# The four token-mixing stages: one float32 product of unsplit operands for each three products of rounded halves

## The chip, the core and the metric

The kernel runs on one core of one Trainium2 chip. The metric is the device time of one execution, in microseconds (us). The engines that matter here are TensorE (PE, with its weight loads PEld), VectorE (DVE), ScalarE (ACT), GpSimd (POOL) and SyncE (SP), whose queue issues nearly all transfers (SPq in the rows).

## The reference

Three blocks follow each other, with B = 2 sequences, H = 8 heads, S = 768 positions, D = 64 (so C = 512 channels):

```python
# 1 attention: a window of 16 around each position, plus 24 block summaries (K: max, V: mean)
scores = concat([mask(q @ k.T / 8), q @ k_sum.T / 8 + log(32)]); a = softmax(scores)
x = (a @ concat([v, v_sum])).reshape(B, S, C)
# 2 mixer: over positions, then over channels
xt = x.transpose(0, 2, 1)
h = relu(xt @ w_tok1) @ w_tok2               # 768 -> 256 -> 768
u = x + h.transpose(0, 2, 1)
x = u + relu(u @ w_ch1) @ w_ch2              # 512 -> 1536 -> 512
# 3 normalisation and MLP
x = x + relu(layernorm(x) * g @ w_ch1) @ w_ch2   # 512 -> 2048 -> 512
```

The weights come as float64 and are turned into float32 in the kernel.

## The kernel before

**Attention** is cut into 24 quads (n = 0 to 23, three for each of the eight head pairs of both sequences; a sequence has 12). A quad makes its scores (PE, L284), subtracts mask and row extremum (DVE, L304), takes the exponential (ACT, L314), transposes (PE, L321), evacuates (ACT, L328), multiplies with V (PE, L341) and normalises into the tile `u`, which holds x for the whole kernel (DVE, L355 and L358). These products are float32.

**Every other product** is made of three products on operands of the rounded type `float32r`: an operand is kept as a rounded part (`h`) and the rest (`l`), and `mm3` (L196 to L200) adds h·h, h·l and l·h in PSUM. The splitting costs one copy (rounded part) and one subtraction (rest) per operand: for `u` in attention an ACT copy (L372, `xh`) and a POOL subtraction (L381, `xl`) per quad; for the hidden layer of token mixing an ACT Relu (L400, `hh`) and a DVE pass (L401, `hl`); for each half of a weight an ACT copy (L175, `wh`) and a DVE subtraction (L182, `wl`).

**Weights** come as 62 halves of 128x512. SP loads one into a `stage` buffer, of which there are three (L165); ACT takes the absolute value of its upper words (L113), and DVE puts the float32 together in four passes (L127, L129, L131, L135; the tile is `dec`). Then the split follows. This chain is a generator (`conversion`, L139) from which pieces are drawn: in attention `convert(ops)` weaves four, later two, DVE steps into each quad's normalisation. It stops when no slot is free. A slot holds two halves with both parts; there are three slots in attention, which is what the six halves of w_tok1 and w_tok2 fill, so no weight of the channel products is converted before attention has ended. Then eight slots are added, and later five more.

**Token mixing** has two stages per sequence. `g1` (L384) makes, for two halves of the channels and two tiles of the hidden layer, 6 products of 128x256 (8 such groups in all). `g2` (L404) makes, for each of 6 tiles of positions, 2 products of 128x512 and adds the result to `u` on DVE (L418; 12 groups). Those of sequence 0 and the g1 of sequence 1 are written into attention, from quad 9 on; the rest follows it, together with transposes of `u`.

**The order.** In attention each step of a quad is put at a due time (the table `ORDER` and the calls of `put`), and PE runs them in just that order. What the other engines run in what order is decided by the tile scheduler within what the program states. From the end of attention to the end, the channel products (`g3`, `g4`) take nearly all of PE, with conversions and transposes beside them.

A loop `fill` (L603) sends small products through PE in the first quads. It is not changed.

Of the kernel before, what the change touches and what calls it, by code (L numbers as in the profile page):

```python
# [52 lines left out]
class Kern:  # L53
# [311 lines left out]
    def att_hi(self, n):  # L365
        nc = self.nc
        i, qd = divmod(n, 3)
        b, p = divmod(i, NPAIR)
        x = self.u[:, b * ST + 2 * qd : b * ST + 2 * qd + 2, p * P : p * P + P]
        hf, c0 = p // 2, (p % 2) * P  # L370
        xh = self.xh[hf][:, 2 * qd : 2 * qd + 2, c0 : c0 + P]
        nc.scalar.copy(xh, x)  # L372

    def att_lo(self, n):
        i, qd = divmod(n, 3)
        b, p = divmod(i, NPAIR)
        hf, c0 = p // 2, (p % 2) * P
        x = self.u[:, b * ST + 2 * qd : b * ST + 2 * qd + 2, p * P : p * P + P]
        xh = self.xh[hf][:, 2 * qd : 2 * qd + 2, c0 : c0 + P]
        xl = self.xl[hf][:, 2 * qd : 2 * qd + 2, c0 : c0 + P]  # L380
        self.nc.gpsimd.tensor_tensor(xl, x, f32(xh), op=ALU.subtract)  # L381
# [465 lines left out]
```

## Time and profile before

| What | Value |
|---|---|
| Time, median of 3 runs | 602.31 us (601.63 to 602.54) |
| The profiled execution: its span (no other time is given of it) | 603.4 us |
| PE busy | 581.6 us, 96% |
| DVE busy | 336.3 us, 56% |
| ACT busy | 211.7 us, 35% |
| POOL busy | 43.6 us, 7% |
| Transfers in | 48.08 MB |

The slices of the profile (15 us each) show four stretches: loading and the first quads, where no engine is full; attention until about 100 us; the end of token mixing until about 128 us; and then 475 us in which PE is at 9 tenths or more. POOL works only in the first 105 us. The transfers run at 230 to 340 GB/s in the first 75 us and at about 100 GB/s after 105 us.

### The profile page before, as it was taken

To read this page: it belongs to the slowest core of one execution; us is meant where nothing else is said; L and a number is where in the kernel's file an instruction comes from. 1 tells how busy PE (TensorE), PEld (TensorE's weight loads), DVE (VectorE), ACT (ScalarE), POOL (GpSimd) and SP (SyncE) were. 2 spreads that over 40 slices of the span, in tenths; PEclk is the share of its full clock that TensorE was granted. 3 is DMA by queue.
4 is the path that set the end of the run, shared out by engine and by line. 5 is a ranking of instruction groups with operands and counts; after the bars stand their busy time and mean duration, and the time that the engine had idled before them with its cause. 6 is when DMAs were issued, how large, how long until landed. Compare 5 with 4: busy or idle time off the path is not lost.

```text
span 603.4 us, 9137 instructions
## 1 busy us (share of the span) xinstructions
PE 581.6 (96%) x3584; PEld 506.2 (84%) x3584; DVE 336.3 (56%) x848; ACT 211.7 (35%) x451; POOL 43.6 (7%) x78
## 2 busy tenths in 40 slices
PE   6777999999999999999999999999999999999997
PEld 2455777789899889899989998998988999989996
DVE  3698976998278899788799931111163211111122
ACT  3988878443233444333444411101122101011010
POOL 0544632000000000000000000000000000000000
PEclk8988999999999999999999999999999999999999
DMA  9979820335034333234323100000010100000011
GB/s 275 338 233 290 271 88 3 104 140 179 31 106 139 105 104 106 94 116 140 114 82 121 35 1 0 1 1 0 1 52 11 44 0 1 0 1 1 0 53 53
DMA packets 21505, 51.81 MB, mean 86 GB/s; under 512 B 2003, under 2 KB 8403, under 8 KB 21462
## 3 DMA queue, kind: packets, MB, share of 16 engines
q1 hardware_dynamic: 21456, 51.21, 26.3%
q8 instruction: 28, 0.46, 0.3%
q14 instruction: 15, 0.12, 0.1%
q10 hardware_dynamic: 6, 0.02, 0.0%
HBM read 48.08 MB, written 3.15 MB: 85 GB/s over the span
## 4 chain that ended last, share of the span: by engine, by line
PE 87%; DMA 5%; DVE 4%; ACT 2%; issue 1%; SPq 1%; DVEq 0%; ACTq 0%
DMA stage<-in_wts_dram 2%; PE g L198 2%; PE g L200 2%; PE g L199 2%; DMA Q<-in_q_dram 1%; DMA V<-in_v_dram 1%; PE av L341 1%; PE pt L321 1%; PE scores L284 1%; PE tx L502 1%; PE tu L435 1%; PE acc_('x', 2)_0_4718 L199 1%; PE acc_('x', 0)_0_3717 L199 1%; PE acc_('x', 2)_1_4719 L200 1%; PE acc_('x', 1)_0_3870 L199 1%; PE acc_('x', 2)_2_4720 L199 1%
## 5 line engine op out<-in xcount | busy, mean ns | idle before, releaser
L131 DVE SCALAR_TENSOR_TENSOR dec<-stage,dec 128x512 uint32<-128x512 uint32 x62 | 44.8, 723 | 0.8
L113 ACT ACTIVATE dec<-stage 128x512 f32<-128x512 f32 x62 | 41.9, 678 | 7.0 <-DMA stage<-in_wts_dram 6.8
L182 DVE TENSOR_TENSOR wl<-dec,wh 128x512 fp32r<-128x512 f32 x62 | 43.2, 699 | 0.0
L135 DVE SCALAR_TENSOR_TENSOR dec<-stage,dec 128x512 uint32<-128x512 uint32 x62 | 42.5, 686 | 0.8
L175 ACT CAST wh<-dec 128x512 fp32r<-128x512 f32 x62 | 38.1, 616 | 12.2 <-DVE dec L135 11.8
L314 ACT ACTIVATE pr<-sn,mn 128x120 f32<-128x120 f32 x96 | 30.8, 385 | 11.8 <-DVE mn L304 11.5
L129 DVE TENSOR_SCALAR dec<-dec 128x512 uint32<-128x512 uint32 x62 | 28.4, 458 | 0.9
L127 DVE TENSOR_SCALAR dec<-dec 128x512 f32<-128x512 f32 x62 | 27.8, 451 | 1.4 <-ACT dec L113 1.3
L284 PE MATMUL scores<-K,Q 64*64 64x120 f32 x384 | 16.7, 292 | 12.1 <-DVE mn L304 7.8
L284 PEld LDWEIGHTS scores<-K,Q 64*64 64x64 f32 x384 | 10.8, 141 | 19.5 <-DVE mn L304 10.5
L304 DVE CUSTOM_DVE_ANT_0 sn<-scores,mask 128x120 f32<-128x120 f32 x96 | 21.7, 274 | 5.5 <-PE scores L284 5.4
L381 POOL TENSOR_TENSOR xl<-u,xh 128x256 fp32r<-128x256 f32 x24 | 19.6, 818 | 27.6 <-ACT xh L372 27.6
L253 POOL TENSOR_TENSOR VT<-VT 128x384 f32<-128x384 f32 (+3 forms) x28 | 18.6, 664 | 30.7 <-DMA VT<-in_vt_dram 29.3
L321 PE MATMUL pt<-ident,pr 128*120 128x128 f32 x96 | 17.7, 308 | 1.0 <-ACT pr L314 1.0
L341 PEld LDWEIGHTS av<-V,PT 121*64 121x64 f32 x384 | 14.2, 145 | 5.3 <-issue 2.6
L341 PE MATMUL av<-V,PT 121*64 121x65 f32 x384 | 17.6, 237 | 0.5 <-POOL VT L253 0.3
L603 PE MATMUL warm_ps<-warm 128*128 128x512 bf16 x48 | 16.5, 455 | 1.2 <-DVE warm L665 1.2
L321 PEld LDWEIGHTS pt<-ident,pr 128*120 128x120 f32 x96 | 12.0, 150 | 6.0 <-ACT pr L314 2.4
L198 PE MATMUL g<-xh,wh 128*128 128x256 f32 x48 | 14.3, 299 | 0.5 <-DVE u L418 0.5
L328 ACT COPY PT<-pt 120x512 f32<-120x512 f32 x24 | 13.9, 579 | 0.4
L477 DVE TENSOR_SCALAR xn<-u,mv,rs 128x128 f32<-128x128 f32 x48 | 14.0, 342 | 0.0
L200 PE MATMUL g<-xh,wl 128*128 128x256 f32 x48 | 13.5, 282 | 0.0
(3004 smaller groups left out, 1677.0 us busy)
## 6 DMA issues: line engine op xcount, KB each, us to landing
stage<-in_wts_dram SPq DMA_DIRECT2D x62, 512.0 KB, 3.3
V<-in_v_dram SPq DMA_DIRECT2D x16, 306.0 KB, 9.0
K<-in_k_dram SPq DMA_DIRECT2D x8, 480.0 KB, 8.2
Q<-in_q_dram SPq DMA_DIRECT2D x8, 384.0 KB, 6.9
VT<-in_vt_dram SPq DMA_DIRECT2D x8, 384.0 KB, 8.2
out_dram<-u SPq DMA_DIRECT2D x12, 256.0 KB, 2.1
mask<-in_mask_dram SPq DMA_DIRECT2D x1, 240.0 KB, 5.3
ident<-in_ident_dram SPq DMA_DIRECT2D x1, 64.0 KB, 5.1
```

What stands on the lines that cost most here:

```text
L113: nc.scalar.activation(m, self.raw[n][:, :, 1].bitcast(F32), AF.Abs)
L129: nc.vector.tensor_scalar(mi, mi, 3, 0x3FFFFFF8, op0=ALU.logical_shift_left, op1=ALU.bitwise_and)
L131: nc.vector.scalar_tensor_tensor(mi, t[:, :, 1], 0xC0000000, mi, op0=ALU.bitwise_and, op1=ALU.bitwise_or)
L135: nc.vector.scalar_tensor_tensor(mi, t[:, :, 0], 29, mi, op0=ALU.logical_shift_right, op1=ALU.bitwise_or)
L175: self.nc.scalar.copy(self.slots[c if c < 16 else c - 16][0][:, s], x)
L182: self.nc.vector.tensor_tensor(wl[:, s], x, f32(wh[:, s]), op=ALU.subtract)
L199: nc.tensor.matmul(out, lhs[0], rhs[1], start=False, stop=False)
L200: nc.tensor.matmul(out, lhs[1], rhs[0], start=False, stop=last)
L284: nc.tensor.matmul(ps[cols, j, e, :NK], Q[rows, 64 * w : 64 * w + 64], K.rearrange("p v c -> p (v c)")[rows, a : a + NK], start=True, stop ...
L314: nc.scalar.activation(pr[:, u], sn[:, u], AF.Exp, bias=mn[:, u : u + 1], scale=-1.0)
L321: nc.tensor.transpose(ps[:NK, u * P : u * P + P], pr[:, u], self.ident)
L341: nc.tensor.matmul(ps[64 * j : 64 * j + 64, e, 65 * r : 65 * r + 65], pt[:, u * P + 64 * (r ^ j) : u * P + 64 * (r ^ j) + 64], V[:, j, 2 * ...
```

## The change

The token weights are decoded into six float32 tiles `tok` and not split; `u` is not split, and g1 reads it as it is; the hidden layer is kept as one float32 tile, made by one ACT Relu; g1 and g2 issue one float32 product where they issued three rounded ones. The tiles of the split parts fall away, and the space goes to slots: five instead of three in attention, then seven and later four. The slots now hold only channel weights, so `conversion` goes on to these (halves 6 to 15) within attention.

```diff
-NHALF = 2 * (3 + F1 + F2)
+NTOK = 6
+NHALF = NTOK + 2 * (F1 + F2)
+NSLOT = 16
...
+        to = self.tok[h].bitcast(U32) if h < NTOK else mi
         nc.vector.scalar_tensor_tensor(
-            mi, t[:, :, 0], 29, mi, op0=ALU.logical_shift_right, op1=ALU.bitwise_or
+            to, t[:, :, 0], 29, mi, op0=ALU.logical_shift_right, op1=ALU.bitwise_or
...
-            if 0 <= h < NHALF and not self.ready(h // 2):
+            if NTOK <= h < NHALF and not self.ready((h - NTOK) // 2):
...
     def split_hi(self, h):
+        if h < NTOK:
+            return
...
     def split_lo(self, h):
+        x = self.dec.pop(h) if self.wide else self.raw.pop(h)
+        if h < NTOK:
+            self.half[h] = self.tok[h]
+            return
...
     def g1(self, b, hf):
-                self.mm3(ps[:, :256], self.tok1(st, t), (xh[:, st], xl[:, st]), st == 0, st == ST - 1)
+                nc.tensor.matmul(
+                    ps[:, :256], self.tok1(st, t), self.u[:, b * ST + st, cs], start=st == 0, stop=st == ST - 1
+                )
             yield
-            nc.scalar.activation(hh, ps[:, :256], AF.Relu)
-            nc.vector.scalar_tensor_tensor(hl, ps[:, :256], 0.0, f32(hh), op0=ALU.max, op1=ALU.subtract)
+            nc.scalar.activation(self.h[b][:, t, cs], ps[:, :256], AF.Relu)
...
     def g2(self, b):
-                self.mm3(ps, self.tok2(t, st), (self.hh[b][:, t], self.hl[b][:, t]), t == 0, t == 1)
+                nc.tensor.matmul(ps, self.tok2(t, st), self.h[b][:, t], start=t == 0, stop=t == 1)
...
-            put(n + O["hi"], lambda n=n: self.att_hi(n))
-            put(n + O["lo"], lambda n=n: self.att_lo(n))
...
-        low = {x0: 5 + O["lo"], x1: 11 + O["lo"], w0: 17 + O["lo"], w1: 23 + O["lo"]}
+        low = {x0: 5 + O["norm"], x1: 11 + O["norm"], w0: 17 + O["norm"], w1: 23 + O["norm"]}
...
-        self.add_slots(slots_a, 3)
+        self.add_slots(slots_a, 5)
...
-        self.add_slots(slots_b, 8)
+        self.add_slots(slots_b, 7)
...
-                self.add_slots(slots_c, 4)
+                self.add_slots(slots_c, 2)
-                self.add_slots(slots_d, 1)
+                self.add_slots(slots_d, 2)
```

Three places show what this moves. Line numbers are each kernel's own: L284, L321, L341, L355, L358 and L304 of before are L298, L335, L355, L369, L372 and L318 of the changed kernel, and the decode passes L127, L129, L131, L135 are L129, L131, L133, L138.

PE, just after the value product of quad 15: the first group of g2 between two quads, before.

```order
L284 MATMUL scores<-K_100,Q_97 64x120 x8
L321 MATMUL pt_1068<-ident,pr_1015 120x128 x4
L341 MATMUL av_1073<-V_104,PT_101 64x65 x8
L198 MATMUL g_0_0_1098<-hh_118,wh_72 128x512
L199 MATMUL g_0_0_1098<-hl_120,wh_72 128x512
L200 MATMUL g_0_0_1098<-hh_118,wl_73 128x512
L198 MATMUL g_0_0_1098<-hh_118,wh_74 128x512
L199 MATMUL g_0_0_1098<-hl_120,wh_74 128x512
L200 MATMUL g_0_0_1098<-hh_118,wl_75 128x512
L284 MATMUL scores<-K_100,Q_97 64x120 x8
```

The same place of the changed kernel.

```order
L298 MATMUL scores<-K_104,Q_101 64x120 x8
L335 MATMUL pt_997<-ident,pr_957 120x128 x4
L355 MATMUL av_1002<-V_108,PT_105 64x65 x8
L397 MATMUL g_0_0_1026<-h_118,tok_123 128x512
L397 MATMUL g_0_0_1026<-h_118,tok_124 128x512
L298 MATMUL scores<-K_104,Q_101 64x120 x8
```

The quads stand where they stood; six rounded products have become two of float32.

DVE, around the normalisation of quad 5 (`rec` and `u` are its two passes, `dec` and `wl` a half's conversion, `sn` the scores of quad 8), before.

```order
L355 RECIPROCAL rec_571<-av_546 128x4
L131 SCALAR_TENSOR_TENSOR dec_458<-stage_398,dec_458 128x512
L358 TENSOR_TENSOR u<-av_546,rec_571 128x2x128
L135 SCALAR_TENSOR_TENSOR dec_458<-stage_398,dec_458 128x512
L182 TENSOR_TENSOR wl_73<-dec_402,wh_72 128x512
L127 TENSOR_SCALAR dec_521<-dec_521 128x512
L227 TENSOR_REDUCE ks_585<-K_98 128x24
L129 TENSOR_SCALAR dec_521<-dec_521 128x512
L304 ISA sn_615,mn_616<-scores,mask 128x120
L304 ISA mn_616 128x1
```

The same place of the changed kernel.

```order
L369 RECIPROCAL rec_560<-av_535 128x4
L372 TENSOR_TENSOR u<-av_535,rec_560 128x2x128
L318 ISA sn_600,mn_601<-scores,mask 128x120
L318 ISA mn_601 128x1
L129 TENSOR_SCALAR dec_453<-dec_453 128x512
L318 ISA sn_600,mn_601<-scores,mask 128x120
L318 ISA mn_601 128x1
```

Five conversion passes that stood between the normalisation and the next scores are gone from this place; four of them stand elsewhere, the subtraction nowhere.

DVE, around the normalisation of quad 18, late in attention, before (`hl` is the rest of the hidden layer).

```order
L355 RECIPROCAL rec_1321<-av_1280 128x4
L358 TENSOR_TENSOR u<-av_1280,rec_1321 128x2x128
L401 SCALAR_TENSOR_TENSOR hl_121<-g_1_0_0_1302,hh_119 128x256
L304 ISA sn_1352,mn_1353<-scores,mask 128x120
L304 ISA mn_1353 128x1
```

The same place of the changed kernel.

```order
L369 RECIPROCAL rec_1233<-av_1204 128x4
L138 SCALAR_TENSOR_TENSOR dec_1142<-stage_1032,dec_1142 128x512
L372 TENSOR_TENSOR u<-av_1204,rec_1233 128x2x128
L192 TENSOR_TENSOR wl_75<-dec_1037,wh_74 128x512
L129 TENSOR_SCALAR dec_1241<-dec_1241 128x512
L192 TENSOR_TENSOR wl_75<-dec_1142,wh_74 128x512
L131 TENSOR_SCALAR dec_1241<-dec_1241 128x512
L129 TENSOR_SCALAR dec_1344<-dec_1344 128x512
L318 ISA sn_1270,mn_1271<-scores,mask 128x120
L318 ISA mn_1271 128x1
```

Here six passes over 128x512 of the channel weights have come in, and the pass for `hl` is gone.

From the scores of quad 4 to those of quad 15 DVE runs 17 one-input passes (TENSOR_SCALAR), 16 merging passes (SCALAR_TENSOR_TENSOR of a half), 6 `wl` and 3 `hl` before, and 15, 15, 2 and 0 after; ACT runs 11 `xh` and 6 `wh` before, 0 and 2 after. From the scores of quad 15 to the last reciprocal DVE runs 2 one-input passes, 4 merging passes, no `wl` and 3 `hl` before, and 13, 14, 5 and 0 after; ACT runs 9 `xh`, no `wh` and no half's L113 before, and 0, 6 and 5 after.

## Rows read from the trace of the kernel before

**Rows 1.** Busy time by stretch: columns as in the first line.
```profile
core 0: us, PE busy (x) PEld busy (x) DVE busy (x) ACT busy (x) POOL busy (x), PEclk, DMA share, GB/s
21.88:67.91 46.03, 36.81 (x479) 26.43 (x481) 42.29 (x155) 39.71 (x99) 23.48 (x36) 0.89 0.93 271
67.91:100.90 32.99, 32.84 (x450) 25.79 (x449) 25.19 (x114) 27.14 (x71) 14.18 (x22) 1.00 0.33 105
100.90:127.90 27.00, 24.82 (x138) 20.96 (x135) 25.58 (x51) 13.83 (x27) 1.47 (x2) 1.00 0.29 97
127.90:350.00 222.10, 222.10 (x1135) 200.49 (x1134) 184.19 (x386) 86.60 (x164) 0.00 (x0) 1.00 0.31 105
350.00:603.40 253.40, 249.30 (x1257) 224.50 (x1255) 50.23 (x103) 33.07 (x67) 0.00 (x0) 1.00 0.04 13
```

**Rows 2.** PE in order of time, columns: start us, us, engine, line, operation.
```profile
47.15 0.28 PE L199 MATMUL g<-xl,wh 128*128 128x256 f32 x1
47.27 0.28 PE L200 MATMUL g<-xh,wl 128*128 128x256 f32 x1
...
74.05 0.39 PE L199 MATMUL g<-hl,wh 128*128 128x512 f32 x1
74.28 0.40 PE L200 MATMUL g<-hh,wl 128*128 128x512 f32 x1
```

**Rows 3.** Lines 284, 341 and 502 on PE: duration ns min/median/max.
```profile
L284 PE MATMUL scores<-K,Q x384: 262/263/460, 6.0 to 96.5; 64*64 64x120 f32 x192
...
L341 PE MATMUL av<-V,PT x384: 219/222/370, 17.0 to 100.8; 121*64 121x65 f32 x192
...
L502 PE MATMUL tx<-ident,xn x48: 270/272/301, 305.1 to 467.4; 128*128 128x128 f32 x48
```

**Rows 4.** The chain, 445 to 449 us: start us, us, what.
```profile
448.75 0.33 PE tx L502 x3
```

**Rows 5.** Groups of DVE and ACT by line: busy us, mean ns, idle before.
```profile
L131 DVE SCALAR_TENSOR_TENSOR dec<-stage,dec 128x512 uint32<-128x512 uint32 x62 | 44.8, 723 | 0.8
L182 DVE TENSOR_TENSOR wl<-dec,wh 128x512 fp32r<-128x512 f32 x62 | 43.2, 699 | 0.0
L129 DVE TENSOR_SCALAR dec<-dec 128x512 uint32<-128x512 uint32 x62 | 28.4, 458 | 0.9
L401 DVE SCALAR_TENSOR_TENSOR hl<-g,hh 128x256 fp32r<-128x256 f32 x8 | 3.4, 419 | 5.1 <-ACT hh L400 5.1
...
L175 ACT CAST wh<-dec 128x512 fp32r<-128x512 f32 x62 | 38.1, 616 | 12.2 <-DVE dec L135 11.8
L372 ACT CAST xh<-u 128x256 fp32r<-128x256 f32 x24 | 9.7, 403 | 1.5 <-DVE u L358 1.3
```

**Rows 6.** DVE and POOL in order of time, 31.5 to 62 us.
```profile
31.89 0.68 DVE L182 TENSOR_TENSOR wl<-dec,wh 128x512 fp32r<-128x512 f32 x1
32.49 1.22 DVE L127 TENSOR_SCALAR dec<-dec 128x512 f32<-128x512 f32 x1
...
61.47 0.73 POOL L381 TENSOR_TENSOR xl<-u,xh 128x256 fp32r<-128x256 f32 x1
61.49 1.25 DVE L182 TENSOR_TENSOR wl<-dec,wh 128x512 fp32r<-128x512 f32 x1
```

**Rows 7.** Waits before 64 us, on SP, ACT and PE, in order of time.
```profile
27.03 10.08 SPq L165 DMA_DIRECT2D stage<-in_wts_dram  x3
...
51.31 0.67 ACT L113 ACTIVATE dec<-stage 128x512 f32<-128x512 f32 x1 [1.43 <-DMA stage<-in_wts_dram]
...
53.70 1.18 PE L321 MATMUL pt<-ident,pr 128*120 128x128 f32 x4 [1.05 <-ACT pr L314]
```

**Rows 8.** PE's waits from 103 to 122 us.
```profile
103.41 0.39 PE L198 MATMUL g<-xh,wh 128*128 128x256 f32 x1 [0.53 <-DVE u L418]
...
118.44 0.50 PE L198 MATMUL g<-hh,wh 128*128 128x512 f32 x1 [0.51 <-DVE u L418]
...
121.31 0.41 PE L198 MATMUL g_('u', 1)_3_1714<-xth_('u', 1)_1664,wh 128*128 128x384 f32 x1 [0.89 <-DVE u L418]
```

More of the change, by code (lines that the diff above doesn't have):

```diff
@@ L186, in weight, with mid @@
         return tuple(w[:, col : col + P] for w in self.half[h])
+    @staticmethod
+    def mid(c):
+        return NTOK + 2 * c
     def tok1(self, st, t):
         col = st * DTOK + t * P
-        return self.weight(col // 512, col % 512)
+        return self.half[col // 512][:, col % 512 : col % 512 + P]
     def tok2(self, t, st):
         col = ST * DTOK + t * S + st * P
-        return self.weight(col // 512, col % 512)
+        return self.half[col // 512][:, col % 512 : col % 512 + P]
     def mm3(self, out, lhs, rhs, first, last):
@@ L363, in att_norm @@
         )
[L365 to L381, printed above, removed]
     def g1(self, b, hf):
         nc = self.nc
-        xh, xl = self.xh[hf], self.xl[hf]
+        cs = slice(256 * hf, 256 * hf + 256)
         for t in range(2):
@@ L537, in g4 @@
             acc = self.acc[g % 2 * GT + j]
-            self.mm3(acc, (a[0][:, s], a[1][:, s]), self.half[2 * c + 1], first, last)
+            self.mm3(acc, (a[0][:, s], a[1][:, s]), self.half[self.mid(c) + 1], first, last)
             if last:
@@ L658, in run @@
         self.gt = const.tile([P, CC], F32, name="gt")
-        self.xh = [xp.tile([P, ST, 256], F32R, name=f"xh{i}") for i in range(2)]
-        self.xl = [xp.tile([P, ST, 256], F32R, name=f"xl{i}") for i in range(2)]
-        self.hh = [xp.tile([P, 2, C], F32R, name=f"hh{i}") for i in range(B)]
-        self.hl = [xp.tile([P, 2, C], F32R, name=f"hl{i}") for i in range(B)]
+        self.h = [xp.tile([P, 2, C], F32, name=f"h{i}") for i in range(B)]
+        self.tok = [xp.tile([P, 512], F32, name=f"tok{i}") for i in range(NTOK)]
         self.warm = att.tile([P, 512], mybir.dt.bfloat16, name="warm")
@@ L709, in run @@
                 units += [(kind, s, f, g) for _, f, g in sorted(order)]
-        last_use = {c: max(n for n, x in enumerate(units) if x[0] == "u" and x[2] == c - 3) for c in range(3, 15)}
+        last_use = {c: max(n for n, x in enumerate(units) if x[0] == "u" and x[2] == c) for c in range(F1)}
         def ready(c):
-            if c < 16:
+            if c < NSLOT:
                 return c < len(self.slots)
-            if c < 19:
-                return xctx is None
-            return n > last_use[c - 16]
+            return n > last_use[c - NSLOT]
         self.ready = ready
@@ L728, in run @@
                 nf = F1 if kind == "u" else F2
-                c = 3 + f if kind == "u" else 3 + F1 + f
-                while 2 * c not in self.half:
+                c = f if kind == "u" else F1 + f
+                while self.mid(c) not in self.half:
                     self.convert_all(4)
@@ L747, in run @@
             if prev is not None:
-                while 2 * prev[1] + 1 not in self.half:
+                while self.mid(prev[1]) + 1 not in self.half:
                     self.convert_all(4)
```

31 lines of the change are left out of this document (9 added, 22 removed).

## The prediction, made blind

> **What bounds the kernel now.** I read the page first (busy shares and slices), then the busy time by stretch, then the order of time in the stretches in which PE is not full, then the groups by line for durations.
>
> The busy time by stretch [rows 1] splits the kernel in four. *Stage A* (21.88 us, scores of quad 4, to 67.91, scores of quad 15): 46.0 us, DVE 42.3 busy, ACT 39.7, PE 36.8, and the transfers at 0.93 of the DMA engines' time. DVE is the fullest engine (0.92). *Stage B* (to 100.90, the last value product): 33.0 us, PE 32.8 busy, DVE 25.2. *Stage C* (to 127.90, token mixing of sequence 1): 27.0 us, PE 24.8, DVE 25.6. *Stage D* (the rest): PE 222.10 of the first 222.10 us. So PE bounds B and D, DVE with its neighbours A, and C is a chain of both. The change touches PE, DVE, ACT and POOL in A to C, and only makes conversions earlier for D.
>
> **PE, the added work.** Rounded products start 0.12 us apart at 256 columns and 0.23 at 512 [rows 2]. The change puts a float32 product in the place of three. Float32 products exist in the kernel: scores and value products show 384 records for 192 products of the program (24 quads by 8 products), so two records for each [rows 3]. A record of 65 columns lasts 222 ns, one of 120 columns 263: (263 - 222) / 55 = 0.75 ns a column. One pitch is seen directly: three transposes of 128 float32 columns in 0.33 us [rows 4], 0.11 us per record, 0.86 ns a column. For 256 columns that is 0.215 us a record as my estimate, between 0.19 (0.75 ns) and 0.22; for 512 it is 0.43 (0.38 to 0.44). A g1 group: 12 x 0.215 - 18 x 0.119 = +0.44 us. A g2 group: 4 x 0.43 - 6 x 0.2327 = +0.32. Over 8 and 12 groups: +3.5 and +3.9, in all +7.4 us of PE (2.8 to 8.3 with the ends). The number of records falls, the time grows. Since PE idles only 9.2 us in A and 2.2 in C, the change must win these back to be worth anything.
>
> **Stage A.** PE: 36.8 + 3 groups x 0.44 = 38.1 us, the floor unless the clock changes. DVE loses, by the counts of the order, 2 one-input passes, 1 merging pass, 4 `wl` and 3 `hl`: 2 x 0.46 + 0.70 + 4 x 0.70 + 3 x 0.42 = 5.7 us [rows 5]. It also loses the company of POOL's 11 subtractions: beside one of them a DVE subtraction lasted 1.25 us instead of 0.68 [rows 6], 0.57 more. If each of 11 hit one DVE pass that would be 6.3 us; I take a third, 2.0, for want of a count. DVE then has 34.6 us of work; at the same busy share (0.92) the stage takes 37.6. ACT loses 11 `xh` x 0.40 and 4 `wh` x 0.62, 6.9 us of 39.7 [rows 5], and so is not the bound. Both limits lie together, PE's 38.1 and DVE's 37.6; I put 39.0, one us over the higher: **-7.0**. The ends: 0, if the transfers or waits for them set the pace (below), and -10, if the clock of PE helps: its mean of 0.89 means that it stood at the lower level (1.2 GHz) for some 22% of the stage, about 10 us, after waits like the one for the exponentials [rows 7]; at the upper level (2.4 GHz) all along, PE's floor would be about 33.
>
> The Trainium skill (page "SBUF — State Buffer", section "SBUF: two separate sides") says that DVE and GpSimd share a port pair as an exclusive lock: a DVE operation with two SBUF inputs and a GpSimd operation that reads SBUF block each other entirely. By that rule up to 11 x 0.82 = 9.0 us of holds would go instead of 2.0, and DVE's work would be up to 7 us lower still. The trace shows 0.57 us of stretching beside a POOL operation of 0.73 [rows 6], so less than the whole of it; and with PE's floor at 38.1 the stage could follow by 0.9 us at most.
>
> **Stage B.** PE has no slack: 33.0 + 3 g1 groups x 0.44 + 4 g2 groups x 0.32 = 35.6, +2.6 (of the 8 g1 groups three lie in A, three here and two in C). DVE gets the conversions: 11 more one-input passes, 10 more merging passes, 5 `wl`, less 3 `hl`. By durations [rows 5]: 11 x 0.46 + 10 x 0.70 + 5 x 0.70 - 3 x 0.42 = +14.2, a tally of 39.4 us; these durations overlap: a subtraction of 0.68 is followed by the next start after 0.60 [rows 6], and by that share (0.60 / 0.70 = 0.86) it is +12.2, 37.4 us. So DVE passes from 25 us to the edge of being the bound. ACT gains 6 `wh` and 5 absolute values but loses 9 `xh`, about +3.4 of 27.1: not the bound. I take **+3.1**, 36.1 us, half a microsecond over PE's 35.6 and short of DVE's 37.4 because passes not done in B can slip past its end, with +2.6 and +6.4 (DVE by durations) as ends.
>
> **Stage C.** PE: 24.8 + 2 x 0.44 + 8 x 0.32 = 28.3 us. Its waits of 2.2 us are for the additions to `u` on DVE [rows 8]; longer products hide most of them. With 0.4 left: 28.7, **+1.7** (+1.3 to +4, if DVE, now with more subtractions from the earlier conversions in its queue, keeps them all).
>
> **Stage D.** PE was full and runs the same products: 0. That conversions are ahead gains nothing where nobody waits for them.
>
> **The sum.** -7.0 + 3.1 + 1.7 + 0 = -2.2 us on the profiled execution of 603.4, its span: 601.2. That execution lies 1.1 above the median of the runs (602.31), so the forecast is 600.1.
>
> **Edits at nothing.** The slots added in attention only allow the conversions counted above; the six `tok` tiles are written by the pass that wrote `dec`; Relu writes one tile as before (0.38 us on ACT); the load instructions on SP are the same 62, and their order past the K, Q and V loads is unchanged but for what waits on `stage` buffers. If that cover fails, it is the first rival.
>
> **Rivals.**
>
> *Transfers pace stage A: slower.* SP waited 10.08 us with weight halves for free `stage` buffers, with loads of K, Q and V behind in the same queue, and ACT waited 1.43 us for a half [rows 7]. ACT works in order: behind an absolute value that waits for its half stand exponentials and evacuations, which PE waits for. The stage moves 271 GB/s x 46.0 us = 12.5 MB; at a share of 1.00 instead of 0.93 that takes 42.8 us, a gain of 3.2 at most, and less where ACT merely waits longer. For it: the 0.93. Against it: the page's second slice moves 338 GB/s, at which 12.5 MB take 37 us, and part of these bytes are for pairs that are used in stage B. With a gain of 2 in A: -2.0 + 3.1 + 1.7 = +2.8, and 605.1. It decides when A gains less than the 4.8 us that B and C cost.
>
> *DVE binds stage B.* Its tally by durations, 39.4 us, holds: -7.0 + 6.4 + 1.7 = +1.1, and 603.4. For it: passes in DVE's queue stand ahead of scores that ACT and PE wait for, as the rows of the order by quad 18 show. Against it: overlapping durations count time twice, and one `dec` or `wl` can wait for a quad more without holding anyone.
>
> *The clock stays up through A*, since PE waits less: -10 + 3.1 + 1.7 = -5.2, and 597.1. For it: longer products and fewer waits. Against it: DVE's 34.6 us of work, and waits like that at 53.70 us, which are for ACT and not for what was removed.
>
> *The float32 product is cheaper than three rounded ones.* If a product were one record at 0.86 ns a column, a g1 group would fall by 2.14 - 1.29 = 0.85 us and a g2 group by 1.40 - 0.86 = 0.54. B would be held by DVE (+3), A by DVE (-7), and C would shrink by about 1: -5, and 597.3. Against it stand the two records for each product [rows 3]. The Trainium skill states such a rule (page "Perfetto Trace Analysis", section "Engine Utilization": the peak rate is halved for FP32_LOW_HIGH), and by it a float32 product would beat three; the trace, with two records at twice the time a column each, bears out a quarter of the rate.
>
> **How the numbers follow.** Forecast 0.40 (600.1, own range 598.5 to 602), transfers 0.28 (605.1), DVE in B 0.14 (603.4), clock 0.14 (597.1), cheaper product 0.04 (597.3). A difference of 0.2%, 1.2 us, is about what a measurement of this kernel can tell from none: faster is below 601.1, slower above 603.5. Faster: 0.30 of the forecast, 0.18 of the last two: 0.48. Same: 0.08 of the forecast, 0.07 of DVE in B and 0.03 of the transfers: 0.18. Slower: the rest, 0.34. The range goes from below the clock case (A at -10, C at its end of +1.3, B at +2.6: 596.2) to just above the transfers case: 595.5 to 606.0.
>
> **What would show it.** Right: float32 records of 512 columns 0.43 us apart, two for each product; quad 15's scores near 61 us instead of 67.9; the last value product near 97; PE full in B and C; the same 475.5 us from the first channel product to the end. Wrong: a float32 product under 0.35 us at 256 columns; quad 15 later than 63.1 (A gains less than 4.8); idle PE in B with DVE named as releaser; or a stage D that is not the same length, which none of my steps allows for.

## The result, and the profile after

The changed kernel takes 606.91 us (median of 6 runs, 604.96 to 609.01), the kernel before 601.97 (6 runs, 601.24 to 603.78): a ratio of 1.0074, with an interval of 1.0051 to 1.0098. It is slower by 4 to 5 us where 2 us of gain were forecast, and the time lies outside the range (595.5 to 606.0).

The profiled execution of the changed kernel has a span of 603.9 us and a time of 605.68; in every run the time is 1.7 to 2.2 us over the span, mostly 1.8. Its busy time by stretch answers to [rows 1], with the stages cut at the same events (scores of quad 4, scores of quad 15, end of the last value product, second channel product of the first unit):

```profile
core 0: us, PE busy (x) PEld busy (x) DVE busy (x) ACT busy (x) POOL busy (x), PEclk, DMA share, GB/s
21.73:61.27 39.54, 34.75 (x455) 24.22 (x457) 34.84 (x150) 32.87 (x83) 11.82 (x24) 1.00 1.04 307
61.27:97.95 36.68, 36.36 (x425) 24.59 (x424) 35.31 (x134) 30.75 (x74) 7.41 (x12) 1.00 0.62 171
97.95:128.22 30.27, 27.70 (x106) 18.05 (x106) 28.80 (x58) 13.54 (x25) 0.00 (x0) 1.00 0.41 139
128.22:603.90 475.68, 471.50 (x2392) 424.90 (x2390) 217.07 (x453) 111.41 (x217) 0.00 (x0) 1.00 0.14 48
```

Beside it the same stages of another execution of the kernel before (run `b_again` below, span 599.5), in which the clock of PE did not drop in stage A:

```profile
21.21:63.93 42.72, 33.20 (x473) 24.04 (x475) 40.98 (x155) 38.91 (x99) 25.33 (x36) 1.00 1.00 298
63.93:97.05 33.12, 32.98 (x451) 25.92 (x450) 25.16 (x114) 27.50 (x71) 13.98 (x22) 1.00 0.33 105
97.05:123.96 26.91, 24.72 (x134) 20.86 (x134) 25.48 (x51) 13.73 (x27) 1.48 (x2) 1.00 0.29 96
123.96:599.50 475.54, 471.40 (x2391) 424.99 (x2389) 234.26 (x488) 119.54 (x231) 0.00 (x0) 1.00 0.17 56
```

D is the same (475.68 and 475.54 us). DVE's work in A fell from 41.0 to 34.8 us, and the stage by 3.2 (against the execution of [rows 1] by 6.5). B and C grew by 3.6 and 3.4.

The chain of waits through stage A, read from 20 to 64 us, changed its owner. Before (`b_again`), by line:

```profile
by line: DVE sn L304 17.0%; DVE dec L131 10.8%; DVE dec L135 10.6%; DVE wl L182 9.7%; issue 9.2%; DVE dec L127 8.0%; DVE u L358 6.7%; DVE dec L129 4.6%; PE pt L321 2.6%; DVE ks L227 2.3%; ACT pr L314 2.2%; PE g L198 2.1%; PE scores L284 2.0
```

After (start us, us, what):

```profile
by line: DMA stage<-in_wts_dram 41.9%; DMA V<-in_v_dram 22.7%; ACT pr L328 9.0%; PE g L385 6.3%; ACT dec L115 5.2%; PE av L355 4.5%; ACT PT L342 3.5%; PE pt L335 2.8%; DVE dec L133 2.7%; DVE dec L129 1.9%; DVE sn L318 1.9%; DVE u L372 1.7%;
...
25.89 10.34 DMA stage<-in_wts_dram
...
39.60 8.11 DMA stage<-in_wts_dram
```

DVE passes made some 70% of the chain before; weight halves that land 8 to 10 us after their issue make 42% of it now, and V loads 23%.

What became of DVE's passes in A can be read from their lines (windows 21.21 to 63.93 of `b_again` and 21.73 to 61.27 of the profile after; mean ns of one behind the comma). Before, with the subtractions `xl` on POOL:

```profile
L131 DVE SCALAR_TENSOR_TENSOR dec<-stage,dec 128x512 uint32<-128x512 uint32 x8 | 7.9, 993 | 0.0
L135 DVE SCALAR_TENSOR_TENSOR dec<-stage,dec 128x512 uint32<-128x512 uint32 x7 | 5.2, 746 | 0.0
L182 DVE TENSOR_TENSOR wl<-dec,wh 128x512 fp32r<-128x512 f32 x6 | 4.7, 777 | 0.0
...
L381 POOL TENSOR_TENSOR xl<-u,xh 128x256 fp32r<-128x256 f32 x11 | 9.7, 882 | 6.4 <-ACT xh L372 6.4
```

After:

```profile
L133 DVE SCALAR_TENSOR_TENSOR dec<-stage,dec 128x512 uint32<-128x512 uint32 x8 | 5.4, 680 | 0.0
...
L138 DVE SCALAR_TENSOR_TENSOR tok<-stage,dec 128x512 uint32<-128x512 uint32 x6 | 4.0, 674 | 0.0
...
L192 DVE TENSOR_TENSOR wl<-dec,wh 128x512 fp32r<-128x512 f32 x1 | 0.7, 672 | 0.0
```

The passes became fewer, and those that stayed became shorter.

How PE's longer products look (after; start us, us, what): a g1 group to the next scores, and a g2 group to the next scores, in stage B.

```profile
63.04 2.86 PE L385 MATMUL g<-u,tok 128*128 128x256 f32 x12
65.83 0.64 PE L298 MATMUL scores<-K,Q 64*64 64x120 f32 x16
...
67.60 1.98 PE L397 MATMUL g<-h,tok 128*128 128x512 f32 x4
69.51 0.64 PE L298 MATMUL scores<-K,Q 64*64 64x120 f32 x16
```

The same two places before, in `b_again`:

```profile
65.70 0.39 PE L198 MATMUL g<-xh,wh 128*128 128x256 f32 x1
...
68.03 0.64 PE L284 MATMUL scores<-K,Q 64*64 64x120 f32 x16
...
69.80 0.50 PE L198 MATMUL g<-hh,wh 128*128 128x512 f32 x1
...
71.39 0.64 PE L284 MATMUL scores<-K,Q 64*64 64x120 f32 x16
```

2.79 against 2.33 us, and 1.91 against 1.59: +0.46 and +0.32, where +0.44 and +0.32 were forecast [rows 2 to 4]. And the records of the float32 products (duration ns min/median/max), two for each product as said of [rows 3]:

```profile
L385 PE MATMUL g<-u,tok x96: 379/379/483, 37.6 to 105.7; 128*128 128x256 f32 x96
...
L397 PE MATMUL g<-h,tok x48: 590/592/697, 67.6 to 128.2; 128*128 128x512 f32 x48
```

The waits of PE in stage C after the change, which answer to [rows 8]:

```profile
100.65 5.45 PE L385 MATMUL g<-u,tok 128*128 128x256 f32 x24 [0.46 <-DVE u L400]
...
111.42 0.50 PE L212 MATMUL acc_('u', 0)_0_1580<-wh,ah_('u', 0)_0_1511 128*128 128x512 f32 x1 [1.20 <-ACT ah_('u', 0)_0_1511 L508]
...
118.22 1.98 PE L397 MATMUL g<-h,tok 128*128 128x512 f32 x4 [0.37 <-DVE u L400]
...
121.08 0.41 PE L212 MATMUL g_('u', 1)_0_1563<-xth_('u', 1)_1525,wh 128*128 128x384 f32 x1 [0.55 <-ACT xth_('u', 1)_1525 L421]
```

The wait for `ah`, the hidden layer of the first channel product, is the new one (0.25 in the executions of the kernel before). The end of the product that `ah` is made of, on PE, and what stands before `ah` on ACT (start us, us, what, idle before):

```profile
109.56 0.34 PE L214 MATMUL g_('u', 0)_0_1498<-xth_('u', 0)_1330,wl 128*128 128x384 f32 x1
...
107.82 0.68 ACT L115 ACTIVATE dec<-stage 128x512 f32<-128x512 f32 x1 [0.77 <-DMA stage<-in_wts_dram]
109.80 0.67 ACT L115 ACTIVATE dec<-stage 128x512 f32<-128x512 f32 x1 [1.30 <-DMA stage<-in_wts_dram]
110.37 0.60 ACT L180 CAST wh<-dec 128x512 fp32r<-128x512 f32 x1
110.88 0.48 ACT L508 ACTIVATE ah_('u', 0)_0_1511<-g_('u', 0)_0_1498 128x384 fp32r<-128x384 f32 x1
```

The product is done at 109.90. ACT takes `ah` up at 110.88, since in its order there stand an absolute value that had waited 1.30 us for its half, and a copy `wh`.

### The profile page after: what moved, and what is told of

It reads as the page before. It is cut to its first block, busy times and chain, and to the rows that moved or that the text cites. A ratio compares the mean times of both kernels' runs of the same rounds, so it can differ in the third digit from the quotient of the medians.

```text
span 603.9 us, 8892 instructions
## 1 busy us (share of the span) xinstructions
PE 587.3 (97%) x3507; PEld 500.5 (83%) x3512; DVE 324.7 (54%) x834; ACT 199.7 (33%) x421; POOL 23.0 (4%) x54
## 3 DMA queue, kind: packets, MB, share of 16 engines
q1 hardware_dynamic: 21456, 51.21, 26.9%
## 4 chain that ended last, share of the span: by engine, by line
PE 82%; DMA 7%; DVE 6%; ACT 3%; issue 1%; SPq 0%; ACTq 0%
DMA stage<-in_wts_dram 4%; PE g L397 2%; DMA V<-in_v_dram 2%; DMA VT<-in_vt_dram 1%; ACT pr L328 1%; DVE sn L318 1%; DVE dec L133 1%; PE tx L484 1%; DMA ident<-in_ident_dram 1%; DVE wl L192 1%; DVE dec L138 1%; PE tu L417 1%; PE acc_('x', 2)_0_4506 L213 1%; PE acc_('x', 0)_0_3505 L213 1%; PE acc_('x', 3)_0_4613 L213 1%; PE acc_('x', 1)_0_3658 L213 1%
## 5 line engine op out<-in xcount | busy, mean ns | idle before, releaser
L133 DVE SCALAR_TENSOR_TENSOR dec<-stage,dec 128x512 uint32<-128x512 uint32 x62 | 42.8, 690 | 0.9
L192 DVE TENSOR_TENSOR wl<-dec,wh 128x512 fp32r<-128x512 f32 x56 | 39.2, 699 | 0.1
L138 DVE SCALAR_TENSOR_TENSOR dec<-stage,dec 128x512 uint32<-128x512 uint32 x56 | 38.3, 685 | 0.8
L180 ACT CAST wh<-dec 128x512 fp32r<-128x512 f32 x56 | 34.4, 614 | 7.7 <-DVE dec L138 7.6
L129 DVE TENSOR_SCALAR dec<-dec 128x512 f32<-128x512 f32 x62 | 26.4, 426 | 3.4 <-ACT dec L115 3.4
L131 DVE TENSOR_SCALAR dec<-dec 128x512 uint32<-128x512 uint32 x62 | 27.4, 442 | 0.9
L318 DVE CUSTOM_DVE_ANT_0 sn<-scores,mask 128x120 f32<-128x120 f32 x96 | 21.5, 274 | 5.4 <-PE scores L298 5.4
L397 PE MATMUL g<-h,tok 128*128 128x512 f32 x48 | 23.0, 605 | 0.4 <-DVE u L400 0.4
L385 PE MATMUL g<-u,tok 128*128 128x256 f32 x96 | 22.5, 386 | 0.5 <-DVE u L400 0.5
L298 PEld LDWEIGHTS scores<-K,Q 64*64 64x64 f32 x384 | 10.7, 142 | 12.9 <-DVE mn L318 5.1
L385 PEld LDWEIGHTS g<-u,tok 128*128 128x128 f32 x96 | 17.7, 190 | 3.3 <-DVE u L400 0.7
L335 PE MATMUL pt<-ident,pr 128*120 128x128 f32 x96 | 17.9, 295 | 2.2 <-ACT pr L328 1.1
L298 PE MATMUL scores<-K,Q 64*64 64x120 f32 x384 | 16.5, 290 | 3.4 <-DVE mn L318 3.4
L335 PEld LDWEIGHTS pt<-ident,pr 128*120 128x120 f32 x96 | 11.5, 142 | 8.9 <-ACT pr L328 4.1
L355 PE MATMUL av<-V,PT 121*64 121x65 f32 x384 | 16.5, 228 | 0.9 <-ACT PT L342 0.3
L355 PEld LDWEIGHTS av<-V,PT 121*64 121x64 f32 x384 | 13.2, 137 | 5.0 <-issue 2.2
L397 PEld LDWEIGHTS g<-h,tok 128*128 128x128 f32 x48 | 8.6, 189 | 7.8 <-issue 6.0
```

The source lines that it names most:

```text
L131: nc.vector.tensor_scalar(mi, mi, 3, 0x3FFFFFF8, op0=ALU.logical_shift_left, op1=ALU.bitwise_and)
L133: nc.vector.scalar_tensor_tensor(mi, t[:, :, 1], 0xC0000000, mi, op0=ALU.bitwise_and, op1=ALU.bitwise_or)
L138: nc.vector.scalar_tensor_tensor(to, t[:, :, 0], 29, mi, op0=ALU.logical_shift_right, op1=ALU.bitwise_or)
L180: self.nc.scalar.copy(self.slots[c % NSLOT][0][:, s], x)
L192: self.nc.vector.tensor_tensor(wl[:, s], x, f32(wh[:, s]), op=ALU.subtract)
L318: self.ttr[n] = nc.vector.tensor_tensor_reduce(sn[:, u], ps[:, u % 2, u // 2, :NK], self.mask[:, mv], scale=-SCALE, scalar=3e38, op0=ALU.a ...
```

## The experiments

Times stand with the runs of the kernel before on the same chip; stages are read from one profiled execution each, PE's clock in A in brackets.

| Run | Time, before beside it | Ratio and interval | A | B | C |
|---|---|---|---|---|---|
| b_again | 602.83, 602.96 | 0.9997 (0.998 to 1.0013) | 42.7 (1.00) | 33.1 | 26.9 |
| a_again | 607.93, 602.96 | 1.0065 (1.0037 to 1.0092) | 41.9 (0.92) | 37.7 | 30.9 |
| cheap_pe | 598.58, 602.96 | 0.9925 (0.9898 to 0.9952) | 41.1 (0.92) | 33.8 | 26.4 |
| late_conv | 605.14, 602.96 | 1.0042 (1.0014 to 1.007) | 39.2 (1.00) | 36.4 | 31.0 |
| a_lite | 608.12, 602.52 | 1.0107 (1.0079 to 1.0135) | 42.2 (0.92) | 38.7 | 29.0 |
| b_lite | 603.35, 602.52 | 1.002 (1.0005 to 1.0035) | 45.1 (0.96) | 33.1 | 26.9 |
| b_f32 | 608.96, 602.52 | 1.0112 (1.0095 to 1.0129) | 44.1 (1.00) | 36.3 | 29.4 |
| mixed | 603.71, 602.52 | 1.0031 (1.0013 to 1.005) | 40.9 (1.00) | 35.7 | 30.6 |
| nohalf | 606.83, 602.65 | 1.0066 (1.0043 to 1.0089) | 40.4 (1.00) | 36.2 | 29.9 |
| early | 607.07, 602.65 | 1.0072 (1.0045 to 1.0098) | 42.8 (0.96) | 36.4 | 30.1 |
| pause | 606.69, 602.65 | 1.0062 (1.0041 to 1.0084) | 40.9 (0.92) | 37.1 | 30.3 |
| one_r | 584.77, 602.65 | 0.9705 (0.9677 to 0.9732) | 39.6 (0.91) | 29.2 | 19.6 |

**Which stage A is usual: b_again, a_again and four more profiled executions.** No edit.

> The kernel before, unchanged. The prediction was made against an execution with a span of 603.4 us, in which PE stood at its lower clock for some 10 us of stage A (scores of quad 4 to scores of quad 15, 46.0 us, mean clock 0.89). Theory 1: that stretch is not in most executions, so a typical one has a stage A of about 43 us and a span near 600, and only about 3.5 us were there to be won. Rival: stage A lasts 46 us again at a clock near 0.9, and what lies between span and time is what differs.

> The changed kernel, unchanged, beside the others on one chip. Theory 1: stages A, B and C (to the second channel product of the first unit) within 1 us of 39.5, 36.0 and 31.0 us, unless the clock drops in A; executions above 606 us are those with a lower mean clock. Rival: the spread is somewhere else, in the loads of the first 22 us or after 128 us.

> The kernel before, one more profiled execution. If the stage A that the prediction started from (46.0 us) is usual, A is 45.5 or more here; if it was one of the slow ones, A lies between 42.7 (no clock drop) and 45, longer with more time at the lower clock.

> As for the other look at the kernel before: stage A between 42.7 and 45 us; B and C at 33.1 and 26.9.

> The changed kernel, one more profiled execution: stage A between 39.5 (no clock drop) and 42, B near 36.7, C near 30.3 (29.9 to 31.0 in those seen so far).

> As for the other look at the changed kernel: stage A between 39.5 and 42 us.

Stage A and its clock, of four executions of each kernel:

| | A (clock) | mean A | mean B | mean C |
|---|---|---|---|---|
| before | 46.0 (0.89), 42.7 (1.00), 45.0 (0.92), 47.5 (0.86) | 45.3 | 33.1 | 26.9 |
| after | 39.5 (1.00), 41.9 (0.92), 41.3 (0.92), 39.5 (1.00) | 40.5 | 37.0 | 31.1 |

The longest and the shortest of before differ by 4.8 us, and its length follows the clock. This is the row of the longest (`b_look2`):

```profile
20.33:67.82 47.49, 38.23 (x472) 28.00 (x474) 40.21 (x156) 38.92 (x98) 24.25 (x37) 0.86 0.99 287
```

So theory 1 of `b_again` is wrong in this: an execution without a clock drop is the rare one, 46.0 was only 0.7 over the mean, and `b_look2`, which was bounded at 45, came out at 47.5. The rival is nearer, but the stage does gain: 4.8 us in the mean. The four profiled executions of before are a little long for the kernel, though: their spans average 601.9 us, a time of some 603.7, where the medians of its runs are 602.0 to 603.0. So 4.8 rather overstates the gain. B and C of the kernel before hardly vary (33.1, and 26.9, in all four); those of the changed kernel do (B 36.5 to 37.7, C 30.3 to 32.6, the last with the clock at 0.95). B of `a_again` (37.7, at a clock of 1.00) and C of `a_look1` lie outside what was expected of them.

**PE's part by itself: b_f32 and cheap_pe.** `b_f32` puts the products alone into the kernel before:

```diff
-self.mm3(ps[:, :256], self.tok1(st, t), (xh[:, st], xl[:, st]), st == 0, st == ST - 1)
+nc.tensor.matmul(ps[:, :256], f32(self.tok1(st, t)[0]), f32(xh[:, st]), start=st == 0, stop=st == ST - 1)
...
-self.mm3(ps, self.tok2(t, st), (self.hh[b][:, t], self.hl[b][:, t]), t == 0, t == 1)
+nc.tensor.matmul(ps, f32(self.tok2(t, st)[0]), f32(self.hh[b][:, t]), start=t == 0, stop=t == 1)
```

> The kernel before with one part of the change alone: each three rounded products of token mixing become one float32 product, of the rounded parts as they lie (the rests are made as before and not used); all work of DVE, ACT, POOL and the transfers stays. Theory 1 (PE pays 8 x 0.45 and 12 x 0.32 us, about 2.6 in B and 3.4 in C, and nothing in A, where DVE sets the pace): slower than before by 5 to 7.5 us. Rival (C's waits for additions swallow a part): slower by 3 to 4 us, with C near 28.7.

Its stages A, B and C:

```profile
19.81:63.90 44.09, 35.20 (x457) 24.20 (x456) 42.35 (x156) 39.06 (x99) 24.98 (x36) 1.00 1.01 299
63.90:100.23 36.33, 35.65 (x425) 24.48 (x424) 25.98 (x113) 27.30 (x71) 14.17 (x22) 1.00 0.30 95
100.23:129.60 29.37, 27.49 (x107) 17.90 (x105) 27.88 (x56) 14.91 (x29) 1.45 (x2) 1.00 0.33 107
```

Its waits of PE in stage C:

```profile
103.01 5.45 PE L390 MATMUL g<-xh,wh 128*128 128x256 f32 x24 [0.53 <-DVE u L410]
...
119.73 1.98 PE L405 MATMUL g<-hh,wh 128*128 128x512 f32 x4 [0.46 <-DVE u L410]
...
122.69 0.41 PE L198 MATMUL g_('u', 1)_3_1582<-xth_('u', 1)_1544,wh 128*128 128x384 f32 x1 [0.65 <-ACT xth_('u', 1)_1544 L431]
```

It is 6.4 us slower than before (1.12%). B costs 3.2 and C 2.5, D is 0.6 longer (476.2), and A, bound by DVE (42.4 of 44.1), lies where it lay. Theory 1 holds: the longer products alone cost more than the whole change does, so all the rest of the change is worth about 2 us (the intervals of the two ratios leave 0 to 5). The rival's swallowed part is small: PE's 2.2 us of waits in C become 1.9 (0.25 for `ah` among them, as before).

`cheap_pe` is the reverse, the changed kernel with PE's work as it was:

```diff
-            for st in range(ST):
+            for st in range(ST - 1):
...
+                n = 512 if t == 0 else 320
-                nc.tensor.matmul(ps, self.tok2(t, st), self.h[b][:, t], start=t == 0, stop=t == 1)
+                nc.tensor.matmul(ps[:, :n], self.tok2(t, st), self.h[b][:, t, :n], start=t == 0, stop=t == 1)
```

> The changed kernel, leaving out the sixth product of each g1 group and the last 192 columns of the second product of each g2 group, so that PE's token mixing costs what it cost before: 5 x 0.43 = 2.15 us for 18 x 0.119 = 2.14, and 0.86 + 0.54 = 1.40 for 6 x 0.2327 = 1.40. Theory 1 (float32 products are paid nearly whole, since PE has no slack in B and C): 5 to 7 us under the changed kernel, so at or below the kernel before. Rival (C is held by waits for additions, conversions and weight halves): 2 to 4 us under the changed kernel, stage C still near 30.

Its stages B and C:

```profile
63.21:97.00 33.79, 33.21 (x419) 23.37 (x418) 33.38 (x130) 30.12 (x74) 6.61 (x12) 1.00 0.62 171
97.00:123.44 26.44, 24.71 (x104) 17.34 (x103) 25.12 (x52) 12.20 (x23) 0.00 (x0) 1.00 0.39 124
```

It is 9.4 us under the changed kernel by the medians (the intervals of the two ratios leave 5 to 12) and 4.4 under the kernel before. B and C are back near 33.1 and 26.9: both stages follow PE's work. In C more went than that work, which fell by 3.0 us: the waits fell too, from 2.6 or more to 1.7. Theory 1 named 5 to 7, the lower part of what was measured; the rival's 2 to 4 are out.

**The early conversions: late_conv and pause.**

```diff
-        self.ready = lambda c: c < len(self.slots)
+        self.ready = lambda c: False
```

> The changed kernel, but no half of the channel weights is converted in attention (float32 products and slots as in the change). Theory (the early conversions put passes in front of what PE waits for in B, and ACT behind weight halves in C): B shorter by 0.5 to 1, C near 28.7, in all 1 to 3 us faster than the changed kernel. Rival (they are what makes C bearable): B the same, C longer by 2 or more, slower than the changed kernel.

B and C:

```profile
60.32:96.71 36.39, 35.84 (x425) 24.55 (x424) 33.36 (x129) 30.86 (x74) 7.01 (x12) 1.00 0.59 169
96.71:127.70 30.99, 28.09 (x107) 18.23 (x107) 29.47 (x59) 12.85 (x24) 0.00 (x0) 1.00 0.38 126
```

B is 0.1 to 1.3 shorter than in the four executions of the changed kernel, C no shorter (31.0). The ratios (1.0042 against 1.0065) have intervals that overlap, so a gain of 2 us is not shown, but the rival, that early conversions are what makes C bearable, is out: without them the time is not longer. The theory is not borne out in C either: the wait for `ah` is there (1.3 us), though no channel weight was converted in attention.

```diff
-            self.convert_all(4)
+            if n >= 2:
+                self.convert_all(5 if n < 12 else 4)
```

> The changed kernel with no conversion step issued beside the first two units of channel products, where token mixing of sequence 1 ends (five steps instead of four in the ten units after). Theory (in C, PE's 2.6 us of waits come from conversions: ACT behind a half that has not landed, DVE's additions behind decode passes): C falls from 30.3 towards 28.3, 1.5 to 2 us faster than the changed kernel. Rival (C is PE's 3.4 us and the chain from addition to transpose): C stays at 30 or more, no difference.

C stayed at 30.3 and so did the new wait:

```profile
113.85 0.50 PE L212 MATMUL acc_('u', 0)_0_1570<-wh,ah_('u', 0)_0_1511 128*128 128x512 f32 x1 [1.24 <-ACT ah_('u', 0)_0_1511 L508]
```

But DVE's work in C stayed too (28.7 us against 28.8): the edit did not take the conversions out of the stage, so it tells nothing of the theory. Other runs tell something: the wait for `ah` is 0.25 again in `nohalf` and `a_lite`, where fewer bytes have to land, but also in `early` below, where all of them do. C is 29.9, 29.0 and 30.1 in these three. So what stands before `ah` on ACT changes from run to run, and the new wait is only a part of what C lost.

**What holds stage A after the change: a_lite, b_lite, nohalf and early.**

```diff
-        queue.dma_start(Q, self.q[b, p])
+        if i < 3:
+            queue.dma_start(Q, self.q[b, p])
```

> The changed kernel, leaving out the loads of Q for pairs 3 to 7 (1.9 MB of the some 12 MB that stage A moves; those scores use an older Q). Theory 1 (with DVE relieved, transfers set the pace of stage A: 307 GB/s at a DMA share of 1.04, and 65% of the chain of waits there is transfers): stage A falls from 39.5 by 2 to 4 us, towards PE's 34.8 of work, B and C unchanged. Rival (DVE and PE set the pace): stage A within 1 us of 39.5.

> The kernel before, with the same loads left out. Theory 1 (before the change DVE sets the pace of stage A, 41.0 of 42.7 us in an execution without a clock drop): stage A stays at 42 to 43 us. Rival (transfers set it there too, share 1.00): it falls by 2 us or more, and the change's relief of DVE was worth nothing from the start.

Neither got faster. For the kernel before that was expected (A 45.1 at a clock of 0.96, among the four above, though not at the 42 to 43 named). For the changed kernel it was not: A took 42.2 us, with a half that ACT awaited for 2.5 us and the clock at 0.92, and B 38.7, the longest of all. The bytes alone are not the pace.

```diff
     def load_half(self, h):
+        if 3 <= h < 12:
+            self.raw[h] = self.kept
+            return
```

> The changed kernel, leaving out the loads of weight halves 3 to 11 (they are decoded from half 0's data, which stays in SBUF). Read in stages A and B only, since later halves have a buffer less. Theory 1 (what holds stage A is ACT's in-order wait for halves that land 8 to 10 us after their issue, behind the loads of a head pair): A falls from 39.5 to 36 to 37.5 us with no wait of ACT or PE for a weight load. Rival (DVE's and PE's own work holds it): A stays at 39 or more.

Stage A, in which ACT now waits 0.4 us for halves in all (2.4 in the changed kernel):

```profile
20.66:61.03 40.37, 35.14 (x455) 24.22 (x457) 39.81 (x154) 34.16 (x84) 18.59 (x34) 1.00 0.96 275
```

It is no shorter, against theory 1. In the place of the transfers stands DVE, at 39.8 of 40.4 us, 5 more than after the change: some passes more fall into the stage (154 instructions for 150), and more of the sums over V on POOL (L273) now run beside its passes and stretch them (18.6 us of POOL in the stage, 11.8 in the changed kernel). POOL and DVE in order of time (start us, us, what):

```profile
31.93 2.55 POOL L273 TENSOR_TENSOR VT<-VT 128x384 f32<-128x384 f32 x3 [4.73 <-DMA VT<-in_vt_dram]
...
31.95 1.27 DVE L131 TENSOR_SCALAR dec<-dec 128x512 uint32<-128x512 uint32 x1
```

A one-input pass of 0.42 us took 1.27 there.

```diff
+            if 2 <= h < 6:
+                t = self.att.tile([P, 512, 2], U32, name=f"early{h}")
...
+        for h, at in ((2, 0.75), (3, 3.7), (4, 5.0), (5, 7.0)):
+            put(at, lambda h=h: self.load_half(h))
```

> The changed kernel with own buffers for token halves 2 to 5 (slots 3, 9, 2, 2 in place of 5, 7, 2, 2), so that their loads are issued without waiting for a free buffer; the same bytes. Theory 1a (the halves are late because they are issued late): A falls from 39.5 to about 37.5, in all 2 to 3 us faster than the changed kernel. Theory 1b (the transfers are at their limit anyway, share 1.04): A stays within 1 us of 39.5, since what the halves gain the loads of the pairs lose.

A took 42.8 us (clock 0.96) and the time is that of the changed kernel: theory 1a is out, and 1b holds in kind, though not in its number (39.5 within 1 us). ACT waits for no half in this stage any more, but PE waits for the sums over V, whose loads take 11.6 us to land in the median (9.4 in the changed kernel; the same wait is 1.3 there):

```profile
30.55 0.42 PE L282 MATMUL psv<-ident,Z 128*120 128x128 f32 x1 [4.53 <-POOL Z L276]
```

So two limits lie within a microsecond or two of each other, transfers with ACT and POOL behind them, and DVE with POOL beside it; taking away one brings out the other. What the stage would be with both gone was not tried.

**Versions: mixed and one_r.** `mixed` keeps float32 in g1 and goes back to three rounded products in g2 (two of its lines):

```diff
-                nc.tensor.matmul(ps, self.tok2(t, st), self.h[b][:, t], start=t == 0, stop=t == 1)
+                self.mm3(ps, self.tok2(t, st), (self.h[b][:, t], self.hl[b][:, t]), t == 0, t == 1)
...
+            nc.vector.scalar_tensor_tensor(hl, ps[:, :256], 0.0, f32(hh), op0=ALU.max, op1=ALU.subtract)
```

> The changed kernel with float32 products in g1 alone; g2 is three rounded products of split operands again (three token halves and the hidden layer are split; four slots in attention). PE pays 8 x 0.45 = 3.6 us instead of 7.4. Theory 1 (what PE pays is paid nearly whole after stage A, and A's extra passes hide under the transfers): 3 to 4.5 us faster than the changed kernel, near or a little over the kernel before. Rival (DVE's passes come back where they hurt): within 1.5 us of the changed kernel.

603.71 us, 0.3% over the kernel before. That is 3.2 under the changed kernel's 606.91 by the medians, as theory 1 had it, and 2.0 to 2.6 by the ratios (1.0031 against 1.0065 and 1.0074), between theory 1 and its rival. The profiled execution does not show where: its C is 30.6, at a clock of 0.94 there.

`one_r` goes the other way, from the kernel before:

```diff
-                self.mm3(ps, self.tok2(t, st), (self.hh[b][:, t], self.hl[b][:, t]), t == 0, t == 1)
+                nc.tensor.matmul(ps, self.tok2(t, st)[0], self.hh[b][:, t], start=t == 0, stop=t == 1)
...
-            put(n + O["lo"], lambda n=n: self.att_lo(n))
```

> The kernel before with a single rounded product in token mixing: only the rounded parts of weights, u and hidden layer are made, the rests and their products are left out (less exact than both kernels; the same values as float32 products of the rounded parts). PE saves 8 x 1.43 and 12 x 0.93 = 22.6 us where the change adds 7.4; DVE and POOL lose what the change takes from them, ACT keeps its copies. Theory 1 (B and C are PE's): B from 33.1 to the 25 to 29 us that DVE and ACT allow, C from 26.9 to 20 to 24, A from 42.7 to about 39.5: 10 to 16 us faster than before. Rival (waits of the chain replace PE's work at once): under 8 us faster.

Stages A, B and C:

```profile
21.07:60.64 39.57, 31.19 (x436) 21.64 (x438) 33.49 (x147) 36.99 (x95) 12.25 (x24) 0.91 1.05 309
60.64:89.80 29.16, 27.23 (x399) 19.77 (x398) 22.20 (x110) 28.04 (x75) 5.92 (x12) 0.94 0.58 143
89.80:109.37 19.57, 17.31 (x87) 13.39 (x86) 18.34 (x36) 10.83 (x22) 0.00 (x0) 1.00 0.16 54
```

584.77 us, 17.9 under the kernel before (3.0%): more than the 10 to 16 expected. PE's work in B and C fell by 5.8 and 7.4 us, and the stages by 4.0 and 7.3; C (19.6) lies a little under the 20 to 24 expected, B (29.2) a little over the 25 to 29, and D is 1.9 shorter, which was not expected. A is as long as after the change (39.6), with the transfers at a share of 1.05 and the clock at 0.91. It beats both kernels, at the price of exactness: `b_f32` and `one_r` keep only the rounded parts.

## Why the prediction was wrong

By the means of four executions of each kernel: A -4.8 (forecast -7.0), B +3.9 (+3.1), C +4.2 (+1.7), D +0.1 (0). Their sum is +3.4 where -2.2 was forecast; the medians of the runs say +4 to +5.

**PE's added work: right.** Two records a product, 0.216 us each at 256 columns (24 in 5.45 us in the first row of the waits in C: less the first record's 0.483, 4.97 for the 23 others), +0.46 and +0.32 a group, +7.5 in all. `b_f32` shows most of it paid (6.4), and `cheap_pe` is in keeping with all of it (5 to 12).

**Stage C: the step that failed most**, by 2.5 us (by 1.9 in the three executions in which the clock stayed up there, 30.6 in the mean against 28.7; PE's work there came to 27.7, 0.6 under the sum). The prediction said of PE's 2.2 us of waits for the additions to `u` [rows 8] that "longer products hide most of them" and left 0.4. `b_f32`, in which the products are longer and nothing else is changed, keeps 1.9, and the changed kernel has 2.6 to 3.3. The three waits for additions sum to 1.93 us before, 1.64 in `b_f32` and 1.38 after. In each of them the longer product stands ahead of what PE waits for, and covers none of it. g1, g2, the transposes and the channel products share two buffers of PSUM (the pool `ps_mm`). At the first and second wait the operands of PE's next product (`u` of the other sequence, or `h`) are there before; the buffer that it needs is still read by the addition, which starts no earlier than the token product ends. At the first, after the change:

```profile
99.90 0.69 DVE L400 TENSOR_TENSOR u<-g,u 128x512 f32<-128x512 f32 x1 [0.35 <-PE g L397]
```

PE goes on at 100.65. At the third wait it is that addition again before, and after the change the copy `xth` of the transposes that follow the token product. What the buffers have to do with it is read from program and rows; a third buffer was not tried. Then a new wait came in, 1.2 to 1.9 us for `ah`, behind a weight half on ACT. The bound of +4 "if DVE keeps them all" named the size, in part with the wrong engine.

**Stage A: mis-sized**, by 2.2 us. DVE's work came out nearly as reckoned, 35.5 us in the mean of four against the 34.6 of the sum, and 5.8 under the 41.3 before, but by other parts. The sum took 5.7 for passes that go. In the windows of the traces one merging pass and one normalisation more fall into A after the change, two `hl` go, not three, and five `wl`, not four: at their usual lengths the passes that go come to 3.6. The company of POOL was worth more than the 2.0 of the sum. Counting for each DVE pass of A that lasted more than 0.15 us over the short ones of its line the time above these, there were 4.9 us before and 1.5 after, in the means of four; 2.0 of the 4.9 lie beside the subtractions `xl`, which is what the term stood for, and those beside the sums over V fell as well. So the nearness of DVE's total is in part luck. By the rule of the Trainium skill (page "SBUF — State Buffer", section "SBUF: two separate sides") up to 9.0 us of holds would have gone with the subtractions; these traces show 2.0.

The term that failed is the "one us over the higher". A lies 3.9 to 5.2 us over the fuller of PE and DVE in the four executions (39.54 against 34.84 in the profile after). In that profile the chain runs through weight halves and V loads, and neither engine sets the pace. PE's work was under the 38.1 of the sum (34.8 to 36.7), as the clock dropped less or not at all, which made up for a part: A was 39.5 at the full clock, 41.3 and 41.9 at 0.92. The rest is the execution that it was measured from, 0.7 over the mean. (The sum also put a span, 603.4, beside a median of times: that execution's time is about 605.2, so it lay 2.9 over the median and not 1.1. The forecast of 600.1 is 2.2 below the median all the same.)

**Stage B: mis-sized**, by 0.8. Of 3.6 us between `b_again` and the profile after, 2.7 are 3 x 0.46 + 4 x 0.32; 0.7 came in the last two quads (from the scores of quad 22 to the end of the last value product 7.8 us after, 7.1 before and in `b_f32`), which the sum had not in view. DVE, at 34.8 to 35.3 of some 37 us, did not bind: `b_f32`, with DVE at 26.0, has the same B less 0.3.

**The rivals.** That the transfers pace A got the nearest time (605.1) and 28%. Its mechanism is half there: the chain through A did pass to weight halves and V loads. But A still gained the 4.8 us that the rival named as the point from which the change breaks even; B and C then took 8.1 and not 4.8. The clock: two of four executions were at 1.00 in A after, one of four before, and each was 1.8 us or more shorter than its like; whether the change raised it, four executions cannot show, and A's end of -10 was not reached. The cheaper float32 product is out by the records.

The range was too narrow above because C's +4 stood in it as the end of a term, and was not added to an A that gains less; both came together. The signs named beforehand for A and PE came true in the profile after (quad 15's scores at 61.27, the last value product done at 97.95); the one that failed is "PE full" in C, 27.7 of 30.3 us.

## What to carry to other kernels

Before a wait is written off as covered by longer work, look whether that work lies on the chain that the wait belongs to: if so, both add up. Cheaper neighbours (DVE, ACT, POOL) are worth what the next limit leaves of them, and longer products in stages where the busy time of PE is the length of the stage are paid nearly in full; one part put alone into the kernel before (`b_f32`) tells these apart in a single run. And a stage whose length varies with the clock by 5 us from one execution to the next is no base for a forecast of 2 us: take several profiles first.
